# Attention and feed-forward on one core: the last visit four steps sooner, and the rows of the last two chunks spread over nine steps

## The chip, the cores and the metric

One core of a Trainium2 chip runs the whole program. The metric is the device time in microseconds (us) of one execution. Engines are named as in the profile: PE is TensorE, DVE is VectorE, ACT is ScalarE, POOL is GpSimd, and SP is the engine whose queue issues most of the DMAs.

## The reference

```
scores = (q @ k.T) / sqrt(64)                 # q, k, v: 8 batches, 8 heads, 576 tokens, 64 wide, fp32
mask   = local (last 32 tokens) for heads 0-3; strided (same position mod 32) for heads 4-7
attn   = softmax(where(mask, scores, -1e9)) @ v
x      = attn.transpose(0, 2, 1, 3).reshape(8, 576, 512)
xn     = (x - mean(x)) / sqrt(var(x) + 1e-6) * g_ln
out    = x + relu(xn @ w_ch1) @ w_ch2         # w_ch1 512x2048, w_ch2 2048x512
```

## The kernel before

The 4608 tokens are cut into nine chunks of 512: chunk b (0 to 7) is the first 512 tokens of batch b, chunk 8 is the 64 left over from each batch. Every matmul of the feed-forward part is done as three fp32r products of a high and a low part (`xh`, `xl`; `hh`, `hl`).

A chunk goes through 16 **steps** f = 0 to 15, one for each 128 of the 2048 hidden columns. In step f, PE does `ffn1` (12 products of 128x512 into the one PSUM bank `ph`), and then the two halves of `ffn2` of step f-1 (12 products into the four sums `po`). ACT makes `hh` from `ph` and DVE makes `hl` from `ph` and `hh`. As there is one `ph` bank, `ffn1` of step f+1 can start once `hl` of step f is made. Each engine executes in the order in which the program was written: the last lines of the kernel chain every instruction to the one before it on its engine.

Attention runs beside this, in **visits** that a generator hands out between `ffn1` and `ffn2`. A pair of heads takes three visits: scores and values (`sv` on PE; mask, maximum and the values' scaling `xo` on DVE; the store of `xo` to the DRAM rows `xdl` and `xds`; a round trip through DRAM in blocks, `sp` and `sx`), then the load of a later `v`, then the turn of the blocks (`pt<-sp` on DVE and others). `slots` says which steps hand out a visit: three of four, all but f % 4 = 1, and one more at f = 9 of the last run. Pair 31, the last, has its one visit in step 11 of the last run (chunk 6), and its store is the last attention result.

Chunks 7 and 8 are then done together in eight **double steps** (`two_steps`) by a scheme of seven products over sums and differences of the two chunks (`t1` to `t4`, `b22`) and of weight blocks (`s` forms, made on POOL by `s_raws`). What it needs is prepared by `coming` within the last steps of chunk 6: load the rows of the two chunks (`x_load`), normalise them (`x_normed`: per tile of 128 rows `bn_stats` and `bn_aggr` on DVE; one power on POOL for all; then one scaling per tile on ACT), turn them on PE into a PSUM bank of a ring of three (`x_turn`, tile `px`), and form the high and low parts (`turn_seventh` for chunk 7, `turn_last` for chunk 8, `more_forms`).

```
at = 2 * f + end - 2 * LAST          # LAST = 11; end is 0 ahead of ffn2, 1 at the step's end
1: free_attention()   2: all 24 loads   3: x_normed(chunk 7)
5: turn_seventh(0, 1), x_normed(chunk 8)      6: turn_seventh(2, 3), s_forms(0)
7: turn_last(0, 1)    8: turn_last(2, 3)      9: more_forms()
```

Of the kernel before, what the change touches and what calls it, by code (L numbers as in the profile page):

```python
# [8 lines left out]
F32 = mybir.dt.float32  # L9
# [3 lines left out]
AF = mybir.ActivationFunctionType  # L13
# [33 lines left out]
def kernel(  # L47
# [10 lines left out]
    nc = tc.nc  # L58
# [46 lines left out]
            tc.tile_pool(name="ps_o", bufs=2, space=bass.MemoryType.PSUM, side="right")))  # L105


    KEPT = 44
    LATE = 120

    ident = keep.tile([P, P], F32, name="ident")
# [634 lines left out]
    def x_t(c):  # L746
        if c not in xt:
            n = c % 2 if c < 2 else (c + 1) % 2
            xt[c] = tuple(xtp.tile([P, NCC, CH], F32R, tag=f"{t}{n}", name=f"{t}{c}")
                          for t in ("xh", "xl"))  # L750
        return xt[c]
# [7 lines left out]
    def x_load(c, i, t=None, halves=(0, 1)):  # L759

        if t is None:
            t = tkp.tile([P, DM], F32, tag="tk", name=f"x{c}_{i}")
        if c < B:
            parts = [(0, P, c, P * i)]
        else:
            parts = [(REST * j, REST, 2 * i + j, CH) for j in range(2)]
        for p0, n, b, r in parts:
            if 0 in halves:
                nc.sync.dma_start(t[p0:p0 + n, 0:DM // 2], xd_l[b][r:r + n, :])
            if 1 in halves:  # L770
                xs = xd_s[b][0:S].rearrange("(r t) d -> t r d", t=NB)
                nc.sync.dma_start(t[p0:p0 + n, DM // 2:DM], xs[r // STR:(r + n) // STR])
        return t
# [8 lines left out]
        nc.gpsimd.tensor_tensor(out=rs, in0=rs, in1=mhalf, op=ALU.pow)  # L782
        return rs

    def x_normed(c, xs):

        mv = stp.tile([P, NT, 2], F32, tag="mv4", name=f"mv{c}", bufs=1)
        rs = stp.tile([P, NT], F32, tag="rs4", name=f"rs{c}", bufs=2)
        for i, x in enumerate(xs):
            st = stp.tile([P, 6], F32, tag="st", name=f"st{c}_{i}")  # L790
            nc.vector.bn_stats(st, x)
            nc.vector.bn_aggr(mv[:, i], st)
        nc.vector.tensor_scalar(rs, mv[:, :, 1], 1e-6, None, op0=ALU.add)
        nc.gpsimd.tensor_tensor(
            out=rs, in0=rs, in1=mhalf.broadcast_to([P, NT]), op=ALU.pow)
        for i, x in enumerate(xs):
            nc.scalar.activation(out=x, in_=x, func=AF.Copy, scale=rs[:, i:i + 1])

    def x_turn(x, name):
        ps = fresh_bank(f"px{name}").rearrange("p (c x) -> p c x", c=NCC)  # L800
        for cc in range(NCC):
            nc.tensor.transpose(ps[:, cc, :], x[:, cc * P:(cc + 1) * P], ident)
        return ps
# [41 lines left out]
    class Run:  # L845
# [11 lines left out]
        def residual(self, f):  # L857

            if not self.last:
                return  # L860
            if self.c < 2:
                i = f - (NFC - NT - 3)
                loads, scales = [i] * (0 <= i < NT), [i - 2] * (1 < i <= NT + 1)
            elif self.c < PLAIN - 1:
                loads = {1: [0], 5: [1], 9: [2], 10: [3]}.get(f, [])
                scales = {5: [0], 9: [1], 13: [2, 3]}.get(f, [])
            else:
                loads = {9: [0], 10: [1], 11: [2], 12: [3]}.get(f, [])
                scales = {11: [0, 1], 13: [2, 3]}.get(f, [])
            for i in loads:  # L870
                x = x_load(self.c, i)
                if self.first:
                    t = None
                else:
                    t = tkp.tile([P, DM], F32, tag="tk", name=f"t{self.c}_{i}")
                    nc.sync.dma_start(t, part[P * i:P * (i + 1), :])
                self.xres.append([x, t])
            for i in scales:
                r = self.xres[i]
                x, t = r  # L880
# [203 lines left out]
    def free_attention():  # L1084
        attn_ctx.close()
        bank_ctx.close()
        pool = late["pool"] = ctx.enter_context(tc.tile_pool(name="late", bufs=1))
        pool.tile([P, LATE], F32, name="late_pad")
        ps_c = ctx.enter_context(tc.tile_pool(name="ps_c", bufs=1, space=bass.MemoryType.PSUM))
        fresh[:] = [(ps_c, f"c{i}") for i in range(3)]  # L1090
        for n in ("t1h", "t1l", "t2h", "t2l"):
            late_tile(n, n)
        late["x"] = []
        for n in ("b22h", "b22l"):
            x = late_tile(n, "x" + n, F32)
            late["x"] += [x[:, 0], x[:, 1]]

    def late_tile(tag, name, dtype=F32R, shape=(P, 2, CH)):
        t = late[name] = late["pool"].tile(list(shape), dtype, tag=tag, name=name)
        return t  # L1100
# [3 lines left out]
    def row_tile(name):  # L1104
        n_rows[0] += 1
        return late_tile(f"r{n_rows[0] % NT}", name, F32, (P, DM))
# [6 lines left out]
    def sub(engine, out, a, b, op=ALU.subtract):  # L1113
        engine.tensor_tensor(out=out, in0=a, in1=b, op=op)  # L1114

    def raw(t):
        return t.bitcast(F32)

    def high_low(hi, lo, src, engine=nc.vector):
        nc.scalar.activation(out=hi, in_=src, func=AF.Copy)  # L1120
        sub(engine, lo, src, raw(hi))

    def turn_seventh(i):
        xh, xl = x_t(B - 1)
        cs = quarter[i]
        high_low(xh[:, :, cs], xl[:, :, cs], x_turn(late["x"][i], f"{B - 1}_{i}"))

    def turn_last(i):
        xh, xl = (raw(t)[:, 0:2, quarter[i]] for t in x_t(B - 1))
        px = x_turn(late["xr"][i], f"{B}_{i}")  # L1130
        t = late["xr"][i].rearrange("p (n c x) -> p n c x", n=2, c=2)
        late["ts"] += [[t[:, 0], t[:, 1]]]
        t1, t2 = late["ts"][i]
        h = [late[n + "h"][:, :, quarter[i]] for n in ("t1", "t2", "b22")]
        l = [late[n + "l"][:, :, quarter[i]] for n in ("t1", "t2", "b22")]
        nc.scalar.activation(out=h[2], in_=px[:, 2:4], func=AF.Copy)
        sub(nc.vector, t1, px[:, 0:2], xh)
        sub(nc.vector, t1, t1, xl)
        sub(nc.vector, t2, px[:, 2:4], t1)
        nc.scalar.activation(out=h[0], in_=t1, func=AF.Copy)  # L1140
        nc.scalar.activation(out=h[1], in_=t2, func=AF.Copy)
        for k, src in ((2, px[:, 2:4]), (0, t1), (1, t2)):
            sub(nc.vector, l[k], src, raw(h[k]))

    def more_forms():

        xh, xl = x_t(B - 1)
        late["t3"], late["t4"] = x_t(B)
        for i in range(NT):
            t1, t2 = late["ts"][i]  # L1150
            cs = quarter[i]
            h, l = (raw(x)[:, :, cs] for x in (xh, xl))
            sub(nc.vector, t1, t2, h[:, 0:2])
            sub(nc.vector, t1, t1, l[:, 0:2])
            sub(nc.gpsimd, t2, h[:, 2:4], t2)
            sub(nc.gpsimd, t2, t2, l[:, 2:4], ALU.add)
        for n, k, engine in (("t3", 0, nc.vector), ("t4", 1, nc.gpsimd)):
            for i in range(NT):
                cs = quarter[i]
                high_low(late[n][:, 0:2, cs], late[n][:, 2:4, cs], late["ts"][i][k], engine)  # L1160

    def coming(f, end):

        at = 2 * f + end - 2 * LAST
        if at == 1:
            free_attention()
        elif at == 2:
            for i, x in enumerate(late["x"]):
                x_load(B - 1, i, x)
            late["xr"] = [x_load(B, i, row_tile(f"xr{i}")) for i in range(NT)]  # L1170
            late["ts"] = []
        elif at == 3:
            x_normed(B - 1, late["x"])
        elif at == 5:
            turn_seventh(0)
            turn_seventh(1)
            x_normed(B, late["xr"])
        elif at == 6:
            turn_seventh(2)
            turn_seventh(3)  # L1180
            late["s"] = s_forms(0)
        elif at == 7:
            for n in ("b22h", "b22l"):
                late_tile(n, n)
            turn_last(0)
            turn_last(1)
        elif at == 8:
            turn_last(2)
            turn_last(3)
        elif at == 9:  # L1190
            more_forms()

    def weight_parts(p):
# [128 lines left out]
        run = two[0].run  # L1322
        return coming_s, [((run, f0, h0), range(NT)), ((run, f1, (hh, hl)), range(NT))]

    LAST = 11
    bank_ctx = ExitStack()
    gen = visits()
    steps = [(r, f) for r in runs for f in range(r.f0, r.f1)]
# [1 line left out]
    slots = {}  # L1330
    for n, (r, f) in enumerate(steps):
        slots[n] = (r is runs[1] and f in (11, 13) or r is runs[2]
                    or r is not runs[1] and (f % 4 != 1 or r is runs[-1] and f == LAST - 2))

    x = hidden[SPLIT - 1]
    prev = runs[0], SPLIT - 1, (x["h"], x["l"])
# [130 lines left out]
```

## Time and profile before

| what | value |
|---|---|
| time, median of 3 runs | 928.41 us (926.06 to 929.92) |
| profiled execution | 929.05 us, its span 927.3 us |
| PE busy | 888.4 us, 96% of the span |
| DVE, ACT, POOL busy | 461.6, 240.3 and 245.0 us |
| granted PE clock, mean of the span | 0.983 |
| chain that ended last | PE 84%, DMA 7%, DVE 2% |

The busy shares are means over the span. In slices of 23 us PE is at 90% or more from the fifth slice to the thirtieth, then at 70, 60, 70 and 60 to 90% in four slices, and again at 90% to near the end. Those four slices are the stage that the change touches.

### The profile page before, as it was taken

The page shows a single profiled execution, that of the slowest core. Times are in us where ns is not written, and L with a number is a line of the kernel's source. Part 1 is how long each engine was busy: PE and PEld are TensorE (multiplying, and loading weights), DVE is VectorE, ACT ScalarE, POOL GpSimd, SP SyncE. Part 2 cuts the span into 40 slices and gives each one's busy share as a digit, 9 for nine tenths or more (in the row PEclk, how much of TensorE's full clock was granted, in tenths as well). Part 3 has the DMA queues.
Part 4 walks back from the last instruction along what each step waited for, and adds up shares of the span by engine and source line. Part 5 has one row for each costly group of instructions (what it writes and reads, how often), then busy time and mean ns, then how long its engine had stood idle before and what let it go on. Part 6 is the DMA issues. An engine that isn't in the chain of part 4 may idle for free.

```text
span 927.3 us, 18356 instructions
## 1 busy us (share of the span) xinstructions
PE 888.4 (96%) x7431; PEld 726.4 (78%) x7431; DVE 461.6 (50%) x859; ACT 240.3 (26%) x429; POOL 245.0 (26%) x301
## 2 busy tenths in 40 slices
PE   6799999999999999999999999999997679999998
PEld 4677888888888888888888888888886458888886
DVE  5886573447744455445554554455434493333300
ACT  4765563112211111111111111111111234333200
POOL 6676385101100000001000100010001458676100
PEclk9999999999999999999999999999998789999999
DMA  9988971247685757575857585756423000000211
GB/s 206 213 184 238 249 204 35 38 102 156 118 160 104 132 92 166 104 132 92 166 104 126 94 157 106 125 97 139 74 70 108 19 26 21 1 0 31 75 49 29
DMA packets 330972, 100.64 MB, mean 109 GB/s; under 512 B 269712, under 2 KB 321800, under 8 KB 330888
## 3 DMA queue, kind: packets, MB, share of 16 engines
q1 hardware_dynamic: 258114, 86.11, 41.7%
q10 hardware_dynamic: 72774, 13.36, 9.5%
q8 instruction: 58, 0.95, 0.4%
q14 instruction: 26, 0.21, 0.1%
HBM read 72.37 MB, written 27.06 MB: 107 GB/s over the span
## 4 chain that ended last, share of the span: by engine, by line
PE 84%; DMA 7%; DVE 2%; SPq 2%; ACT 1%; POOL 1%; issue 1%; POOLq 0%; DVEq 0%; ACTq 0%
PE po L836 39%; PE ph L811 30%; PE u L1234 5%; PE sv L659 4%; PE v L1234 2%; DMA s<-in_moe_w_ch_dram 2%; DMA rows<-in_k_dram 2%; DMA xr<-xds 1%; DVE xr L1114 1%; PE c L1234 1%; DMA v_l<-in_v_dram 1%; POOL sr L1114 1%; DMA x<-xds 1%; PE px L690 1%; DMA v_s<-in_v_dram 0%
## 5 line engine op out<-in xcount | busy, mean ns | idle before, releaser
L836 PE MATMUL po<-w,hh 128*128 128x512 f32 x1024 | 321.2, 395 | 0.7 <-DVE hl L822 0.7
L811 PE MATMUL ph<-xh,w 128*128 128x512 f32 x880 | 292.9, 394 | 1.1 <-DVE hl L822 1.1
L836 PEld LDWEIGHTS po<-w,hh 128*128 128x128 f32 x1024 | 189.9, 188 | 40.5 <-ACT pt L503 0.8
L822 DVE SCALAR_TENSOR_TENSOR hl<-ph,hh 128x512 fp32r<-128x512 f32 x112 | 77.5, 692 | 280.4 <-ACT hh L817 280.4
L836 PE MATMUL po<-w,hl 128*128 128x512 f32 x512 | 200.0, 391 | 0.0
L811 PEld LDWEIGHTS ph<-xh,w 128*128 128x128 f32 x880 | 166.9, 190 | 36.4 <-DVE hl L822 1.5
L811 PE MATMUL ph<-xl,w 128*128 128x512 f32 x440 | 172.4, 392 | 0.0
L817 ACT ACTIVATE hh<-ph 128x512 fp32r<-128x512 f32 x112 | 66.8, 596 | 336.9 <-PE ph L811 265.1
L488 POOL TENSOR_TENSOR sm<-sm,mx 128x640 f32<-128x640 f32 (+1 forms) x32 | 40.7, 1270 | 372.0 <-issue 211.8
L836 PEld LDWEIGHTS po<-w,hl 128*128 128x128 f32 x512 | 96.5, 189 | 20.5
L811 PEld LDWEIGHTS ph<-xl,w 128*128 128x128 f32 x440 | 83.5, 190 | 17.0
L782 POOL TENSOR_TENSOR rs<-rs,mhalf 128x1 f32<-128x1 f32 x28 | 15.4, 551 | 144.6 <-DVE rs L781 117.3
L493 ACT ACTIVATE sm<-sm 128x640 f32<-128x640 f32 (+1 forms) x32 | 23.8, 742 | 105.7 <-POOL sm L488 105.7
L836 PE MATMUL po<-w,h 128*128 128x512 f32 x186 | 42.3, 389 | 0.0
L1114 POOL TENSOR_TENSOR sr<-sr,w 128x256 f32<-128x256 f32 x48 | 40.0, 833 | 3.8
L836 PEld LDWEIGHTS po<-w,h 128*128 128x128 f32 x186 | 34.9, 188 | 7.2
L1114 POOL TENSOR_TENSOR s<-sr,s 128x256 fp32r<-128x256 f32 x32 | 24.4, 794 | 23.3 <-ACT s L1220 23.3
L239 DVE SCALAR_TENSOR_TENSOR p<-s,p 128x512 uint32<-128x512 uint32 x32 | 22.0, 689 | 11.7 <-ACT p L235 11.6
L484 DVE TENSOR_REDUCE mx<-sm 128x10 f32<-128x640 f32 (+1 forms) x32 | 26.3, 822 | 1.9
L1114 DVE TENSOR_TENSOR x<-po,x 128x512 f32<-128x512 f32 x8 | 5.3, 689 | 39.6 <-PE po L836 29.9
L671 DVE TENSOR_TENSOR xo<-sv,den 128x256 f32<-128x256 f32 (+1 forms) x72 | 24.0, 389 | 0.0
L229 ACT ACTIVATE s<-s 128x512 f32<-128x512 f32 x32 | 21.4, 671 | 6.2 <-DMA s<-in_moe_w_ch_dram 6.2
(194 smaller groups left out, 996.4 us busy)
## 6 DMA issues: line engine op xcount, KB each, us to landing
s<-in_moe_w_ch_dram SPq DMA_DIRECT2D x32, 512.0 KB
out_dram<-x SPq DMA_DIRECT2D x32, 256.0 KB
raw<-in_q_dram SPq DMA_DIRECT2D x104, 72.0 KB
raw<-in_k_dram ACTq DMA_DIRECT2D x68, 72.0 KB
xdl<-xo SPq DMA_DIRECT2D x16, 256.0 KB
x<-xdl SPq DMA_DIRECT2D x32, 128.0 KB
x<-xds SPq DMA_DIRECT2D x32, 128.0 KB
wd<-sm SPq DMA_DIRECT2D x10, 384.0 KB
```

Source lines behind the costliest of these rows:

```text
L239: nc.vector.scalar_tensor_tensor(out=self.p[i], in0=self.bits(i), scalar=3, in1=self.p[i], op0=ALU.logical_shift_left, op1=ALU.bitwise_or)
L484: engine(self.mx[:, :, 0:nt], self.smv, axis=AX.X)
L488: nc.gpsimd.tensor_tensor(out=sm, in0=sm, in1=mx[:, :, 0:nt].unsqueeze(3).broadcast_to([P, 2, nt, w]), op=ALU.subtract)
L493: nc.scalar.activation(out=self.smv, in_=self.smv, func=AF.Exp, scale=SCALE)
L659: nc.tensor.matmul(dst, at, by, start=True, stop=True, tile_position=pos)
L671: nc.vector.tensor_tensor(out=xot[0:n, :, t0:t1], in0=src, in1=pv.den[0:n, :, t0:t1].unsqueeze(3).broadcast_to([n, 2, t1 - t0, D]), op=ALU ...
L811: nc.tensor.matmul(ph, w[:, cc], x[:, cc, :], start=(n + k == 0), stop=(n == NCC - 1 and k == 2))
L817: nc.scalar.activation(out=hh, in_=ph, func=AF.Relu)
L822: nc.vector.scalar_tensor_tensor(out=hl, in0=ph, scalar=0.0, in1=hh.bitcast(F32), op0=ALU.max, op1=ALU.subtract)
L836: nc.tensor.matmul(po, hx[:, cs], w, start=(start and n == 0), stop=(stop and n == 2))
L1114: engine.tensor_tensor(out=out, in0=a, in1=b, op=op)
L1234: nc.tensor.matmul(po, a[:, c], b[:, c, :], start=(start and c + k == 0), stop=(stop and c == 1 and k == 2), skip_group_check=True)
```

## The change

`LAST` becomes 7, and the visits that `slots` left out are handed out in the steps behind step 7 of chunk 5 and in all of chunk 6, so pair 31 is visited in step 7. `coming` is spread over steps 3 to 15. Three tiles of chunk 8 (batches 0 to 5) are loaded in steps 3 to 5 and normalised at the end of step 6; the local halves of three more tiles are loaded in step 6; what needs the last store is loaded at the end of step 7; the fourth tile of chunk 8 and the four of chunk 7 are normalised together at the end of step 10. Chunk 8 is turned first and copied by ACT to the row tiles `ts`; `turn_seventh` then forms its sums and differences with chunk 7's `px` in PSUM as one operand.

```diff
-    KEPT = 44
+    KEPT = 36
...
             else:
-                loads = {9: [0], 10: [1], 11: [2], 12: [3]}.get(f, [])
-                scales = {11: [0, 1], 13: [2, 3]}.get(f, [])
+                loads = {7: [0], 9: [1], 14: [2, 3]}.get(f, [])
+                scales = {13: [0, 1], 15: [2, 3]}.get(f, [])
...
+    def turn_last(i):
+        px = x_turn(late["x8"][i], f"{B}_{i}")
+        h, l = (late["b22" + k][:, :, quarter[i]] for k in "hl")
+        nc.scalar.activation(out=h, in_=px[:, 2:4], func=AF.Copy)
+        nc.scalar.copy(out=late["ts"][i], in_=px.rearrange("p (n c) x -> p n c x", n=2))
+        sub(nc.vector, l, px[:, 2:4], raw(h))
...
-        xh, xl = x_t(B - 1)
         cs = quarter[i]
-        high_low(xh[:, :, cs], xl[:, :, cs], x_turn(late["x"][i], f"{B - 1}_{i}"))
...
+        px = x_turn(late["x"][i], f"{B - 1}_{i}")
+        xh, xl = (t[:, :, cs] for t in x_t(B - 1))
+        t1, t2 = (late["ts"][i][:, n] for n in range(2))
+        h, l = ([late[n + k][:, :, cs] for n in ("t1", "t2")] for k in "hl")
+        nc.scalar.activation(out=xh, in_=px, func=AF.Copy)
+        sub(nc.vector, t1, t1, px[:, 0:2])
+        sub(nc.vector, t2, t2, t1)
         nc.scalar.activation(out=h[0], in_=t1, func=AF.Copy)
         nc.scalar.activation(out=h[1], in_=t2, func=AF.Copy)
-        for k, src in ((2, px[:, 2:4]), (0, t1), (1, t2)):
-            sub(nc.vector, l[k], src, raw(h[k]))
+        sub(nc.vector, xl, px, raw(xh))
+        sub(nc.vector, l[0], t1, raw(h[0]))
+        sub(nc.vector, l[1], t2, raw(h[1]))
+        sub(nc.vector, t1, t2, px[:, 0:2])
+        sub(nc.vector, t2, px[:, 2:4], t2)
...
     def more_forms():
-            sub(nc.vector, t1, t2, h[:, 0:2])
-            sub(nc.vector, t1, t1, l[:, 0:2])
-            sub(nc.gpsimd, t2, h[:, 2:4], t2)
-            sub(nc.gpsimd, t2, t2, l[:, 2:4], ALU.add)
...
-        at = 2 * f + end - 2 * LAST
...
+        at = f + 0.5 * end - LAST
...
+        if at == -4:
+            late["x8"] = tiles(NT, f"x{B}")
+            late["x"] = tiles(2, f"x{B - 1}")
+        elif at in (-3.5, -2.5, -1.5):
+            i = int(at + 3.5)
+            x_load(B, i, late["x8"][i])
+        elif at == -1:
+            for i, x in enumerate(late["x"]):
+                x_load(B - 1, i + 2, x, (0,))
+            x_load(B, NT - 1, late["x8"][NT - 1], (0,))
+        elif at == -0.5:
+            x_normed("a", late["x8"][0:3])
+        elif at == 0.5:
             free_attention()
+            x_load(B, NT - 1, late["x8"][NT - 1], (1,))
+            for i, x in enumerate(late["x"]):
+                x_load(B - 1, i, x, (0, 1) if i < 2 else (1,))
...
+        elif at == 3.5:
+            x_normed("b", late["x8"][3:] + late["x"])
...
-    LAST = 11
+    LAST = 7
...
-                    or r is not runs[1] and (f % 4 != 1 or r is runs[-1] and f == LAST - 2))
+                    or r is not runs[1] and (
+                        f % 4 != 1 or r is runs[-1] or r is runs[-2] and f > LAST))
```

The turns: `turn_last(0)` and `(1)` at the start of step 9, `(2)` in 10, `(3)` with `turn_seventh(0)` in 12, `turn_seventh(1)` at the end of 12, `(2)` with `s_forms(0)` in 13, `(3)` in 14, `more_forms` in 15. The raw forms `sr` of `s_forms` share their SBUF space with the first two tiles of chunk 7 (`xs`).

On ACT, before, steps 12 to 14 of chunk 6 (`hh_12` to `hh_14`; `xb22h` and `xb22l` hold the four tiles of chunk 7, `xr` those of chunk 8):

```order
L817 ACTIVATE hh_12_7714<-ph_12_7701 128x512
L797 ACTIVATE xb22h<-xb22h,rs_7762 128x512 x2
L797 ACTIVATE xb22l<-xb22l,rs_7762 128x512 x2
L817 ACTIVATE hh_13_7794<-ph_13_7781 128x512
L1120 ACTIVATE xh_7824<-px_0_7826 128x4x128
L1120 ACTIVATE xh_7824<-px_1_7833 128x4x128
L797 ACTIVATE xr_7726<-xr_7726,rs_7841 128x512
```

On ACT, now, steps 10 to 12 (`x_3_7308` is the fourth tile of chunk 8; `xs` and the two behind it are chunk 7):

```order
L818 ACTIVATE hh_10_7707<-ph_10_7694 128x512
L1127 ACTIVATE b22h<-px_2_7711 128x2x128
L1128 COPY xr_7599<-px_2_7711 128x512
L798 ACTIVATE x_3_7308<-x_3_7308,rsb 128x512
L798 ACTIVATE xs_7607<-xs_7607,rsb 128x512
L798 ACTIVATE xs_7608<-xs_7608,rsb 128x512
L798 ACTIVATE x_0_7309<-x_0_7309,rsb 128x512
L798 ACTIVATE x_1_7310<-x_1_7310,rsb 128x512
L818 ACTIVATE hh_11_7768<-ph_11_7755 128x512
L818 ACTIVATE hh_12_7797<-ph_12_7784 128x512
```

The scalings stood in two groups of four ahead of `hh_13` and `hh_14`; the second group now is five long and stands ahead of `hh_11`.

On DVE, before, from the turn of pair 31's blocks (`pt`) in step 10 to the last visit's scaling (`xo`) in step 11:

```order
L573 RECIPROCAL den_3_7588<-den_3_7588 128x12
L737 STREAM_TRANSPOSE pt_3_7592<-sp_3_7522 128x768
L822 SCALAR_TENSOR_TENSOR hl_11_7624<-ph_11_7609,hh_11_7622 128x512
L671 TENSOR_TENSOR xo_3_7649<-sv_3_7626,den_3_7588 128x2x3x64
L671 TENSOR_TENSOR xo_3_7649<-sv_3_7626,den_3_7588 128x2x2x64
```

On DVE, now, the same place in steps 6 and 7 (`sta` and `mva` are the statistics of three tiles of chunk 8):

```order
L573 RECIPROCAL den_3_7487<-den_3_7487 128x12
L737 STREAM_TRANSPOSE pt_3_7491<-sp_3_7416 128x768
L792 BN_STATS sta_7511<-x_0_7305 128x6
L793 BN_AGGR mva<-sta_7511 128x2
L792 BN_STATS sta_7514<-x_1_7306 128x6
L793 BN_AGGR mva<-sta_7514 128x2
L792 BN_STATS sta_7517<-x_2_7307 128x6
L793 BN_AGGR mva<-sta_7517 128x2
L794 TENSOR_SCALAR rsa<-mva 128x3
L823 SCALAR_TENSOR_TENSOR hl_7_7540<-ph_7_7525,hh_7_7538 128x512
L671 TENSOR_TENSOR xo_3_7565<-sv_3_7542,den_3_7487 128x2x3x64
```

The statistics of three tiles now stand between the turn and `hl` of the next step, ahead of the last visit's `xo`.

On SP's queue, now, from the last store `xds_218<-xo` in step 7 (`x_0_7583` is a residual row tile of chunk 6):

```order
L554 DMA xds_218<-xo_3_7565 54x5x128
L769 DMA x_0_7583<-xdl_209 128x256
L772 DMA x_0_7583<-xds_217 128x1x256
L772 DMA x_3_7308<-xds_217 64x1x256
L772 DMA x_3_7308<-xds_218 64x1x256
L769 DMA xs_7607<-xdl_210 128x256
L772 DMA xs_7607<-xds_218 128x1x256
L769 DMA xs_7608<-xdl_210 128x256
L772 DMA xs_7608<-xds_218 128x1x256
L772 DMA x_0_7309<-xds_218 128x1x256
L772 DMA x_1_7310<-xds_218 128x1x256
```

Before, the same store was followed by one residual tile, 8 loads of chunk 7 and 16 of chunk 8; now 8 loads of the two chunks stand behind it.

## Rows read from the trace of the kernel before

**Rows 1.** Busy time by stretch: steps 13 to 15 with the first double step; the second.
```profile
core 0: us, PE busy (x) PEld busy (x) DVE busy (x) ACT busy (x) POOL busy (x), PEclk, DMA share, GB/s
703.87:769.38 65.51, 44.32 (x159) 33.80 (x158) 38.17 (x75) 21.56 (x48) 30.65 (x40) 0.79 0.14 48
769.38:784.37 14.99, 14.99 (x68) 12.39 (x66) 5.00 (x7) 5.49 (x11) 11.24 (x15) 1.00 0.01 2
```

**Rows 2.** Timeline of PE: start, us, instruction, count, [idle before and its releaser].
```profile
694.73 0.92 PE L659 MATMUL sv<-v_s,pt 54*64 54x64 f32 x44
...
714.17 1.97 PE L802 MATMUL px<-ident,xb22h 128*128 128x128 f32 x8 [4.70 <-ACT xb22h L797]
...
726.58 0.66 PE L802 MATMUL px<-ident,xb22l 128*128 128x128 f32 x4 [4.45 <-DVE xl L1114]
727.00 1.03 PE L836 MATMUL po<-w,hh 128*128 128x512 f32 x2
...
730.72 0.63 PE L836 MATMUL po<-w,hh 128*128 128x512 f32 x2
...
741.66 1.03 PE L802 MATMUL px<-ident,xr 128*128 128x128 f32 x8
742.45 0.71 PE L836 MATMUL po<-w,hh 128*128 128x512 f32 x2
...
747.09 0.47 PE L1234 MATMUL c<-xh,w 128*128 128x512 f32 x1 [1.66 <-ACT t2h L1141]
...
758.91 0.80 PE L1234 MATMUL u<-t2h,s 128*128 128x512 f32 x1 [3.84 <-ACT p L1239]
...
762.57 2.93 PE L1234 MATMUL u<-xh,s 128*128 128x512 f32 x6 [0.73 <-ACT u L1239]
```

**Rows 3.** The chain that ended last, around the last visit: start, us, what.
```profile
692.08 2.73 PE ph L811 x12
694.83 0.61 ACT hh L817
...
696.07 1.08 DVE xo L671 x3
...
697.51 3.40 DMA xds<-xo
...
705.95 6.35 DMA xr<-xds
```

**Rows 4.** Timeline of DVE, steps 10 to 15 and the first double step.
```profile
690.09 0.69 DVE L822 SCALAR_TENSOR_TENSOR hl<-ph,hh 128x512 fp32r<-128x512 f32 x1 [4.75 <-ACT hh L817]
...
691.93 0.98 DVE L737 STREAM_TRANSPOSE pt<-sp 128x768 f32<-128x768 f32 x1
...
727.04 0.68 DVE L791 BATCH_NORM_STATS2 st<-xr 128x6 f32<-128x512 f32 x1
...
730.60 0.17 DVE L793 TENSOR_SCALAR rs<-mv 128x4 f32<-128x4 f32 x1
734.97 0.69 DVE L822 SCALAR_TENSOR_TENSOR hl<-ph,hh 128x512 fp32r<-128x512 f32 x1 [4.20 <-ACT hh L817]
...
740.09 0.45 DVE L1114 TENSOR_TENSOR xr<-xr,xl 128x256 f32<-128x256 f32 x1
...
750.58 0.96 DVE L1114 TENSOR_TENSOR xr<-xr,xh 128x256 f32<-128x256 f32 x1
```

**Rows 5.** Timeline of ACT, the scaling of chunk 8's four tiles.
```profile
731.90 2.56 ACT L797 ACTIVATE xr<-xr,rs 128x512 f32<-128x512 f32 x4 [14.49 <-POOL rs L794]
```

**Rows 6.** Timeline of POOL: powers of one and of four columns, and two subtractions.
```profile
718.31 0.55 POOL L782 TENSOR_TENSOR rs<-rs,mhalf 128x1 f32<-128x1 f32 x1 [4.95 <-DVE rs L781]
...
730.84 1.02 POOL L794 TENSOR_TENSOR rs<-rs,mhalf 128x4 f32<-128x4 f32 x1 [4.22 <-DVE rs L793]
...
738.84 3.00 POOL L1114 TENSOR_TENSOR s<-sr,s 128x256 fp32r<-128x256 f32 x4
750.42 0.84 POOL L1114 TENSOR_TENSOR xr<-xh,xr 128x256 f32<-128x256 f32 x1 [8.58 <-issue]
```

**Rows 7.** Timeline of SP's queue: one load's issue.
```profile
701.38 0.52 SPq L772 DMA_DIRECT2D xb22h<-xds  x1
```

More of the change, by code (lines that the diff above doesn't have):

```diff
@@ L783, in x_scale, with x_normed @@
         return rs
-    def x_normed(c, xs):
-        mv = stp.tile([P, NT, 2], F32, tag="mv4", name=f"mv{c}", bufs=1)
-        rs = stp.tile([P, NT], F32, tag="rs4", name=f"rs{c}", bufs=2)
+    def x_normed(name, xs):
+        n = len(xs)
+        mv = stp.tile([P, NT + 1, 2], F32, tag="mv5", name=f"mv{name}", bufs=1)
+        rs = stp.tile([P, NT + 1], F32, tag="rs5", name=f"rs{name}", bufs=2)
         for i, x in enumerate(xs):
-            st = stp.tile([P, 6], F32, tag="st", name=f"st{c}_{i}")
+            st = stp.tile([P, 6], F32, tag="st", name=f"st{name}_{i}")
             nc.vector.bn_stats(st, x)
             nc.vector.bn_aggr(mv[:, i], st)
-        nc.vector.tensor_scalar(rs, mv[:, :, 1], 1e-6, None, op0=ALU.add)
+        nc.vector.tensor_scalar(rs[:, 0:n], mv[:, 0:n, 1], 1e-6, None, op0=ALU.add)
         nc.gpsimd.tensor_tensor(
-            out=rs, in0=rs, in1=mhalf.broadcast_to([P, NT]), op=ALU.pow)
+            out=rs[:, 0:n], in0=rs[:, 0:n], in1=mhalf.broadcast_to([P, n]), op=ALU.pow)
         for i, x in enumerate(xs):
@@ L1090, in free_attention @@
         fresh[:] = [(ps_c, f"c{i}") for i in range(3)]
-        for n in ("t1h", "t1l", "t2h", "t2l"):
+        late["ts"] = [row_tile(f"xr{i}").rearrange("p (n c x) -> p n c x", n=2, c=2)
+                      for i in range(NT)]
+        for n in ("t1h", "t1l", "t2h", "t2l", "b22h", "b22l"):
             late_tile(n, n)
[L1093 to L1096, printed above, removed]
+        late["x"][0:0] = [late_tile(f"s{i}", f"xs{i}", F32, (P, DM)) for i in range(2)]
     def late_tile(tag, name, dtype=F32R, shape=(P, 2, CH)):
@@ L1128, in turn_last @@
[L1128 to L1139, printed above, removed]
+        px = x_turn(late["x"][i], f"{B - 1}_{i}")
@@ L1145, in more_forms @@
+        sub(nc.vector, l[0], t1, raw(h[0]))
+        sub(nc.vector, l[1], t2, raw(h[1]))
+        sub(nc.vector, t1, t2, px[:, 0:2])
+        sub(nc.vector, t2, px[:, 2:4], t2)
     def more_forms():
-        xh, xl = x_t(B - 1)
         late["t3"], late["t4"] = x_t(B)
[L1149 to L1152, printed above, removed]
-            sub(nc.vector, t1, t2, h[:, 0:2])
-            sub(nc.vector, t1, t1, l[:, 0:2])
-            sub(nc.gpsimd, t2, h[:, 2:4], t2)
-            sub(nc.gpsimd, t2, t2, l[:, 2:4], ALU.add)
@@ L1159, in more_forms, with tiles @@
                 cs = quarter[i]
-                high_low(late[n][:, 0:2, cs], late[n][:, 2:4, cs], late["ts"][i][k], engine)
+                high_low(late[n][:, 0:2, cs], late[n][:, 2:4, cs], late["ts"][i][:, k], engine)
     def coming(f, end):
-        at = 2 * f + end - 2 * LAST
-        if at == 1:
+        at = f + 0.5 * end - LAST
+        def tiles(n, name):
+            return [tkp.tile([P, DM], F32, tag="tk", name=f"{name}_{i}") for i in range(n)]
+        if at == -4:
[11 more added lines that the diff above has]
+        elif at == 0.5:
             free_attention()
+            x_load(B, NT - 1, late["x8"][NT - 1], (1,))
+            for i, x in enumerate(late["x"]):
+                x_load(B - 1, i, x, (0, 1) if i < 2 else (1,))
         elif at == 2:
[L1168 to L1171, printed above, removed]
+            turn_last(0)
+            turn_last(1)
         elif at == 3:
-            x_normed(B - 1, late["x"])
+            turn_last(2)
+        elif at == 3.5:
+            x_normed("b", late["x8"][3:] + late["x"])
         elif at == 5:
+            turn_last(3)
             turn_seventh(0)
+        elif at == 5.5:
             turn_seventh(1)
-            x_normed(B, late["xr"])
         elif at == 6:
             turn_seventh(2)
-            turn_seventh(3)
             late["s"] = s_forms(0)
         elif at == 7:
[L1183 to L1186, printed above, removed]
+            turn_seventh(3)
         elif at == 8:
-            turn_last(2)
-            turn_last(3)
-        elif at == 9:
             more_forms()
```

## The prediction

> **What bounds the kernel now.** I first read the busy shares: PE works for 96% of the span, so time can only be won where PE waits or runs slowly. The slices of the span put that in one place, the last steps of chunk 6 and the first double step. There I took the busy time by stretch, from the first product of step 13 to the first of the second double step, and then PE's timeline for the waits in it. The reader is to see two things. The stretch takes 65.51 us, at a mean granted clock of 0.79; the double step behind it takes 14.99 us, PE is busy for all of it and the clock is 1.00 [rows 1]. And the long waits of PE end on work of `coming`: 4.70 us for chunk 7's scaled tiles, 4.45 us for a PSUM bank that DVE had not read out, 3.84 us for an ACT copy queued behind the high parts of `more_forms` [rows 2].
>
> How much is there to win? Twelve products take 2.73 us [rows 3]. Three steps are six such groups, 16.4 us. Eight turned tiles take 0.40 us each: two of them start at 741.66 and the next product at 742.45 [rows 2]. The first double step has 12 products fewer than the second, 14.99 - 2.73 = 12.3 us [rows 1]. Together 31.9 us at full clock, so the stretch loses 65.5 - 31.9 = **33.6 us**, in waits and in clock.
>
> What starts it all is the last store: `xds<-xo` follows its `xo` at once and takes 3.40 us, and a load of rows issued at 705.95 takes 6.35 us more [rows 3]. Statistics, power, scaling, turning and forming then follow one another while PE has nothing else.
>
> **The change part by part.** The visits keep their number and their work on PE, and the last one comes four steps, some 22 us, sooner. The loads, the turns and the formings keep their sizes; DVE loses eight 256-wide subtractions and gains four, POOL loses eight, ACT gains four copies of 512. These lie beside 5.5 us of products a step and cost nothing as long as `hl` of each step is made in time, for that is what the next `ffn1` waits for. So I look at each step for what now stands ahead of `hh` on ACT and of `hl` on DVE. Let E be the end of a step's `ffn1`. Undisturbed, `hh` (0.61) and `hl` (0.69) are done at E + 1.34, counting the small gaps [rows 3, 4].
>
> *The normalising as a chain.* For four tiles it is to be read whole: statistics from 727.04 to 730.77, power 1.02, scaling 2.56, then `hh` and `hl`, which ends at 735.66 [rows 4 to 6]: 8.6 us. Per tile that is 0.89 on DVE and 0.64 on ACT, plus 0.16 on POOL for each column (0.55 for one, 1.02 for four). Three tiles make 2.84 + 0.87 + 1.92 + 1.30 = 6.9 us, five make 4.62 + 1.18 + 3.20 + 1.30 = 10.3 us, from the first statistic to the end of the next step's `hl`.
>
> *Three tiles, end of step 6.* They begin when the turn of pair 31's blocks is over. That turn ends at 692.91, 2.13 us after its step's `hl` (690.78) [rows 4]. So `hl` of step 7 is done at E + 1.34 + 2.13 + 6.9 = E + 10.4. PE needs it at E + 3 x 2.73 + 0.92 (the last `sv` [rows 2]) = E + 9.1. **New wait at step 8: 1.3 us.** The last `xo` stands behind this `hl` and is late by nearly as much.
>
> *Five tiles, end of step 10.* They begin behind one low part of 0.45 [rows 4], so `hl` of step 11 is done at E + 1.8 + 10.3 = E + 12.1. PE needs it at E + 3 x 2.73 + 0.4 = E + 8.6. **New wait at step 12: 3.5 us.** It is the wait of before in a smaller form: the five scalings stand ahead of `hh` of step 11 in ACT's order.
>
> *The clock behind it.* After the wait of 4.45 us PE's rows stay long until 730.72, and the granted clock of the stretch says why: the lower of its two levels, 1.2 GHz for 2.4. 4.1 us at half speed lose **2.1 us**. After 1.66 us the row is not long (0.47 against 0.80 behind 3.84 us) [rows 2]. So I charge it behind the 3.5 us and not behind the 1.3 us. Bounds: 0, and twice that, for behind 758.91 the rows are long still past the next wait (2.93 for six at 762.57).
>
> *Forming, steps 12 and 13.* Let T be the end of `ffn1` of step 12. DVE owes `hl` (T + 1.34), a low part and two `turn_seventh` of one 512-wide (0.69) and six 256-wide (0.45) subtractions each, 3.4 us a tile, before `hl` of step 13, which so ends at T + 9.3. PE needs it at T + 3 x 2.73 + 4 x 0.4 = T + 9.8. There is no wait if nothing is slower. But POOL makes the raw forms at that very time, because their space is freed when chunk 7's first tiles are turned. With POOL busy, one subtraction of two SBUF operands took 0.96 (beside POOL's row at 750.42), another 0.45 (within POOL's row at 738.84) [rows 4, 6]. Six of the fourteen have two SBUF operands. At +0.5 each that is 3.0 - 0.5 = 2.5 us of wait; at none, 0. I take the middle, **1.2 us**, as the rows show both.
>
> The Trainium skill (SBUF — State Buffer, section "SBUF: two separate sides") says that DVE with two SBUF inputs and POOL share a port pair as an exclusive lock, held for a whole instruction. The row of 0.96 agrees with it; by that rule the 0.45 should not stand where it does. By the rule alone the term would be 2.5 or more in place of 1.2; its worst case is a rival below.
>
> *The first double step.* Its 3.84 us go: the copy `p` stood behind POOL's and DVE's extra forms, which are now done at `turn_seventh`. The 0.73 us for the copy of `u` stay, since nothing is put between them [rows 2]: **0.7 us**.
>
> *Late rows.* From E of step 6: `xo` and the store's issue at E + 11.8, landed at + 3.4, eight loads of 0.54 each behind it, the last landed 6.35 later [rows 3, 7]: E + 26.0. The five statistics run from E + 26.7 to E + 31, the last tile's from E + 30. They are covered, with some 4 us to spare.
>
> **The sum.** 1.3 + 3.5 + 2.1 + 1.2 + 0.7 = 8.8 us stay of 33.6, so 24.8 us go. The profiled execution took 929.05 us, 0.6 us above the median of the runs shown: 929.05 - 24.8 = 904.2, by the median 903.6. I say **904 us**; with the bounds of the clock and of the forming, 900 to 908.
>
> **The rivals.** (A) is that forecast.
>
> (B) The normalising is hidden: no wait at steps 8 and 12. 904.2 - 1.3 - 3.5 - 2.1 = 897. For it speaks that DVE and ACT are half idle; against it, that ACT's order holds `hh` behind the scalings and that in the kernel before just this chain is seen in full.
>
> (C) By the rule on the port pair each of the six subtractions waits for a whole instruction of POOL, 0.84: 5.0 - 0.5 = 4.5 us at step 14 and 2.1 for the clock, in place of 1.2: 910. Against it is the row of 0.45.
>
> (D) The rows come late: from 4 us of delay on, each us is one of wait at step 12. Loads that need twice 6.35 us give 2 to 6 us: 906 to 910. Against it, 10 loads now stand behind the store instead of 26.
>
> (E) The other side: visits three steps apart. From pair 26 to 31 five intervals lose a step. The block round trip (`sp`, for pairs 26 and 27 `sx` as well) and the q and k loads must land in that much less; if not, DVE waits in front of `pt` and `hl` is behind it. From 5 us a pair, about 3 of wait and 2.1 of clock, the 24.8 us are gone: 929 or more. Against it: pair 31 already follows pair 30 after three steps, and its `pt` starts without a wait at 691.93 [rows 4]; that interval has no `sx` and no loads, though. In part, 1 to 2 us a pair, it gives 909 to 914.
>
> That the last visit does not come sooner is excluded by the order of the instructions.
>
> **How the numbers follow.** Chances: A 0.60, B 0.12, C 0.07, D 0.07, E in part 0.09, E in full 0.05. The range 896 to 911 takes in A, B, C, D and a little of E. About 0.5%, 4.6 us, is what a measurement of this kernel can tell from no change (its three runs lie 3.9 us apart). All but E in full are faster by more: faster 0.95; of the rest, same 0.02, slower 0.03.
>
> **What would show it.** Right: in the profile after, PE has a wait of about 1.3 us for `hl` at step 8 and one of 3 to 4 us at step 12, rows of half speed behind the second only, no wait on `px` for PSUM or for scaled tiles, and 0.7 us at `u` in the first double step. Step by step: ACT scales five tiles directly ahead of `hh` of step 11. Wrong: statistics that wait for a DMA at the end of step 10 (D), subtractions of 1 us or more beside POOL and a wait at step 14 over 2.5 us (C), PE waiting at `sv` or for `hl` in chunk 5 (E), or no wait at step 12 at all (B). If the double steps behind the first grow longer than 14.99 us, the change has cost where I saw none.

## The result and the profile after

The changed kernel took 914.0 us (median of 4 runs, 912.42 to 916.03) against 928.61 (926.06 to 929.92): ratio 0.985, 95% interval 0.9815 to 0.9879. It is faster by 14.6 us, not by the 24.8 us forecast, and lies outside the range. The profiled execution is the slowest of the four (916.03, span 914.2).

First the stretches: three behind the waits outside the tail, then step 13 to the end of the first double step, then the second. They are the busy times by stretch (columns as in [rows 1]).

```profile
621.93:626.00 4.07, 4.07 (x11) 3.26 (x12) 3.97 (x10) 0.63 (x1) 0.00 (x0) 0.59 0.81 127
689.03:693.50 4.47, 4.47 (x13) 3.52 (x14) 0.93 (x3) 0.00 (x0) 0.00 (x0) 0.62 0.37 100
717.23:721.30 4.07, 4.07 (x11) 3.21 (x12) 0.00 (x0) 0.00 (x0) 0.00 (x0) 0.58 0.00 0
725.65:756.38 30.73, 30.00 (x137) 24.42 (x136) 23.85 (x52) 13.70 (x33) 20.56 (x28) 1.00 0.15 52
756.38:771.37 14.99, 14.99 (x68) 12.41 (x67) 5.16 (x7) 5.60 (x12) 11.24 (x16) 1.00 0.01 2
```

The stretch that took 65.51 us [rows 1] now takes 30.73, at full clock: of PE's waits nothing is left in it but 0.73 us. (2.4 us of the difference are six turned tiles that now stand ahead of it, at the 0.40 us each of the prediction.) The second double step is unchanged at 14.99. So the gain was had, and part of it given back earlier. PE's waits after the first 100 us (us in total, times, longest) say where:

```profile
PE ph L812 <- DVE hl L823: 9.2, 3, 3.8
PE u L1242 <- ACT u L1247: 0.7, 1, 0.7
```

And PE's timeline gives the places (columns as in [rows 2]): in front of step 14 of chunk 5 and of steps 8 and 12 of chunk 6, with the first product of step 14 behind them.

```profile
621.93 0.79 PE L812 MATMUL ph<-xh,w 128*128 128x512 f32 x1 [2.25 <-DVE hl L823]
...
689.03 0.50 PE L812 MATMUL ph<-xh,w 128*128 128x512 f32 x1 [3.81 <-DVE hl L823]
...
717.23 0.65 PE L812 MATMUL ph<-xh,w 128*128 128x512 f32 x1 [3.14 <-DVE hl L823]
...
731.71 0.40 PE L812 MATMUL ph<-xh,w 128*128 128x512 f32 x1
```

All three long waits are for `hl`, and behind each some 4 us run at a granted clock of about 0.6, part of the time at the lower of the two levels (1.2 GHz for 2.4). Duration times one minus the clock prices that: 4.07 x 0.41, 4.47 x 0.38 and 4.07 x 0.42, 1.7 us each. So 9.2 + 5.1 = 14.3 us stand outside the stretch.

What held `hl` is read one engine back, on ACT, which makes `hh` ahead of it:

```profile
611.62 0.60 ACT L818 ACTIVATE hh<-ph 128x512 fp32r<-128x512 f32 x1 [1.53 <-PE ph L812]
614.91 5.54 ACTq L419 DMA_DIRECT2D v_s<-in_v_dram  x6
620.56 0.60 ACT L818 ACTIVATE hh<-ph 128x512 fp32r<-128x512 f32 x1 [8.34 <-DMA sp<-wd]
...
685.83 1.95 ACT L798 ACTIVATE x<-x,rsa 128x512 f32<-128x512 f32 x3 [9.14 <-POOL rsa L795]
687.68 0.57 ACT L818 ACTIVATE hh<-ph 128x512 fp32r<-128x512 f32 x1
...
712.80 0.72 ACT L798 ACTIVATE x<-x,rsb 128x512 f32<-128x512 f32 x1 [5.97 <-POOL rsb L795]
713.43 1.32 ACT L798 ACTIVATE xs<-xs,rsb 128x512 f32<-128x512 f32 x2
714.66 1.32 ACT L798 ACTIVATE x<-x,rsb 128x512 f32<-128x512 f32 x2
715.88 0.57 ACT L818 ACTIVATE hh<-ph 128x512 fp32r<-128x512 f32 x1
```

At steps 8 and 12 it is the scalings, directly ahead of `hh`, as foreseen. In chunk 5 it is something else: six v loads that ACT itself issues ahead of `hh` of step 13. The first goes out at 614.91, 2.7 us after the `hh` of 611.62 is done, and the six take 5.54 us. The issues themselves are short, as the trace's account of line 419 there shows (in ns, least, median and most; then the first and last start, in us):

```profile
L419 ACTq DMA_DIRECT2D v_s<-in_v_dram x6: 279/280/337, 614.9 to 620.2; - x6
```

That is some 1.7 us of the 5.54. The rest is waiting: by the semaphore events of the trace each issue was released by the landing of a load of the same visit's blocks, an `sx` load for the first four and an `sp` load for the last two. In ACT's order `hh` stands behind the last of them.

Such a group isn't new, nor is its length. ACT before, in chunk 4:

```profile
475.95 0.60 ACT L817 ACTIVATE hh<-ph 128x512 fp32r<-128x512 f32 x1 [4.84 <-PE ph L811]
476.22 5.16 ACTq L419 DMA_DIRECT2D v_s<-in_v_dram  x6
481.48 0.60 ACT L817 ACTIVATE hh<-ph 128x512 fp32r<-128x512 f32 x1 [4.94 <-PE ph L811]
```

There the six took 5.16 us, but they began while the `hh` ahead of them was still at work, and the next `hh` was 0.1 us late. In chunk 5 `hh` is 3.5 us late (idle 8.34 us for 4.84), and 2.7 of these are the late start.

Why step 8 waits 3.81 us and not 1.3 is seen on DVE and on SP's queue. DVE first:

```profile
680.59 0.70 DVE L792 BATCH_NORM_STATS2 sta<-x 128x6 f32<-128x512 f32 x1 [0.26 <-DMA x<-xdl]
...
683.74 0.69 DVE L792 BATCH_NORM_STATS2 sta<-x 128x6 f32<-128x512 f32 x1 [2.24 <-DMA x<-xds]
...
688.28 0.69 DVE L823 SCALAR_TENSOR_TENSOR hl<-ph,hh 128x512 fp32r<-128x512 f32 x1 [3.42 <-ACT hh L818]
```

The statistics of the second and third x8 tile waited 0.26 and 2.24 us for their rows. SP's queue shows where the loads had stood:

```profile
671.77 2.03 SPq L722 DMA_DIRECT2D sp<-wd  x4
673.85 0.54 SPq L769 DMA_DIRECT2D x<-xdl  x1
...
677.67 0.53 SPq L772 DMA_DIRECT2D x<-xds  x1
```

SP issues in the order of the program. The eight loads of those two tiles, from 673.85 to 678.2, stand behind the `sp` loads of pair 30's visit in step 4, which read pair 31's blocks and had to wait for them to be stored. Nothing in those rows depends on it. The last of the eight goes out at 677.67, and its statistic starts at 683.74.

### The profile page after: what moved, and what is told of

Read it like the earlier page. It is cut to its first block, busy times and chain, and to the rows that moved or that the text cites. A ratio compares the mean times of both kernels' runs of the same rounds, so it can differ in the third digit from the quotient of the medians.

```text
span 914.2 us, 18339 instructions
## 1 busy us (share of the span) xinstructions
PE 885.7 (97%) x7431; PEld 725.0 (79%) x7431; DVE 455.6 (50%) x855; ACT 241.8 (26%) x433; POOL 238.6 (26%) x293
## 4 chain that ended last, share of the span: by engine, by line
PE 87%; issue 5%; DMA 3%; SPq 2%; ACT 2%; DVE 1%; POOL 0%; ACTq 0%; DVEq 0%; POOLq 0%
PE po L837 40%; PE ph L812 30%; PE u L1242 5%; PE sv L659 4%; PE v L1242 2%; PE c L1242 1%; SPq L722 1%; DMA x<-xds 1%; PE px L690 1%; DMA rows<-in_k_dram 1%; PE av L514 1%; PE pp L498 1%; PE av L523 0%; DMA sp<-wd 0%; PE t L377 0%
## 5 line engine op out<-in xcount | busy, mean ns | idle before, releaser
L292 POOL TENSOR_TENSOR w<-r,w 128x512 fp32r<-128x512 f32 x16 | 20.6, 1294 | 8.4 <-ACT w L288 8.3
```

## The experiments

The first four kernels below stand beside 7 runs of the kernel before (928.61 us, 927.69 to 932.95), the last three beside 11 more (928.56 us, 925.70 to 931.29). A ratio is to that kernel before.

**e1_again.** The changed kernel once more, not a character altered.

> The changed kernel itself, a second time, for a second profile. In the first one TensorE stood idle in the first 35 us for 2.57 and 4.17 us in the middle of a run of equal matmuls, with no releaser, and the steps of chunk 1 came about 4 us later than in the kernel before, though nothing was changed there. Theory 1 (this differs from execution to execution): here the steps of chunk 1 come at another time, by 2 us or more, and the time lies near 912 to 916. Theory 2 (it belongs to the changed program): the same two idle times, the steps again 4 us late.

912.22 us (909.07 to 913.59, 4 runs), ratio 0.9808 (0.9777 to 0.9839). The profiled execution took 909.07, 7 us less than the first one. It has the same three waits, of 2.54, 3.28 and 3.15 us; but the busy times by stretch behind them (columns as above) show the slow clock behind the third alone:

```profile
617.29:621.40 4.11, 3.97 (x88) 3.03 (x88) 4.01 (x10) 1.23 (x2) 0.00 (x0) 1.00 0.79 126
682.47:687.00 4.53, 4.53 (x20) 3.74 (x21) 1.63 (x4) 0.60 (x1) 0.00 (x0) 1.00 0.38 101
709.08:713.20 4.12, 4.12 (x10) 3.29 (x11) 0.00 (x0) 0.00 (x0) 0.00 (x0) 0.50 0.00 0
```

That is some 3 us of the 7: 5.1 against 4.12 x 0.50 = 2.1. Most of the rest lies in the first 35 us, where the first trace has PE idle in the middle of equal matmuls with no releaser:

```profile
19.02 0.31 PE L445 MATMUL sp<-kt_l,qt_l 64*32 64x64 f32 x1 [2.57 <-issue]
...
31.38 0.65 PE L514 MATMUL av<-v_l,pt 64*32 64x65 f32 x21 [4.17 <-issue]
```

The second execution of the same program has 0.30 us at the first place and nothing at the second:

```profile
17.68 0.24 PE L445 MATMUL sp<-kt_l,qt_l 64*32 64x64 f32 x1 [0.30 <-issue]
```

So this idle, and the clock behind the first two waits, belong to an execution, not to the change. The other kernels below have 0.55 to 2.59 us at the first place. The variants are compared with 912.2.

**e2_rows_early.** The twelve loads of the first three x8 tiles are asked for at the end of step 3, ahead of pair 30's loads in SP's queue.

```
-        elif at in (-3.5, -2.5, -1.5):
-            i = int(at + 3.5)
-            x_load(B, i, late["x8"][i])
+        elif at == -3.5:
+            for i in range(3):
+                x_load(B, i, late["x8"][i])
```

> The 12 loads of the first three tiles of chunk 8 are all issued at the end of step 3, ahead of the visit of step 4 on SP's queue, in place of one tile each at the ends of steps 3, 4 and 5. Theory (the second and third tile stood behind that visit's block loads on SP and landed after their statistics were due): no statistic waits for a DMA at the end of step 6, the wait at step 8 falls from 3.8 to 1.3 to 1.5 us and no slow rows follow it: 3.5 to 4 us faster than the changed kernel. Rival (the loads land late whatever stands ahead of them, or the wait at step 8 is the scaling's alone): the wait stays above 3 us, no gain.

907.54 us (905.70 to 907.59, 4 runs), ratio 0.9758 (0.9731 to 0.9784). DVE's second and third statistic follow the first without a wait, and PE's wait at step 8 falls from 3.28 to 1.13 us; first DVE, then PE:

```profile
674.21 0.70 DVE L792 BATCH_NORM_STATS2 sta<-x 128x6 f32<-128x512 f32 x1
...
675.04 0.66 DVE L792 BATCH_NORM_STATS2 sta<-x 128x6 f32<-128x512 f32 x1
```

```profile
680.30 0.50 PE L812 MATMUL ph<-xh,w 128*128 128x512 f32 x1 [1.13 <-DVE hl L823]
```

With the rows in time, the wait is the prediction's own: 1.3 us forecast, 1.13 measured, at full clock. The edit moves the time by 4.7 us; 2.15 of that is the wait, and the rest may be the clock behind it, slow in some executions of the changed kernel and not in others.

**e3_v_on_sp.** All v loads that ACT issued go out on SP's queue. The edit takes in more than the stall: 18 groups, the first at 262 us in the trace before, and not the last visits alone. PE waited at none of the other 17.

```
-                pairs[i + 2].load_v(queue=nc.scalar if by_blocks else nc.sync)
+                pairs[i + 2].load_v(queue=nc.sync)
```

> The loads of v in the last visits are issued from SP's queue and not from ScalarE's. Theory (in chunk 5 hh of step 13 stood behind six DMA issues of ScalarE that took 5.5 us, as they now come one step behind the block loads and wait for them): the wait of 2.25 us in chunk 5 and the slow rows behind it go, 4 us faster than the changed kernel. Rival (the visits are too close for their block loads or their q and k loads, so VectorE is late in front of pt or of the transposes): the wait stays or comes elsewhere in chunk 5.

908.19 us (907.74 to 908.99, 4 runs), ratio 0.977 (0.9745 to 0.9795): 4.0 us less than e1_again. PE does not wait in chunk 5, and ACT's `hh` there is released by PE, 4.84 us after ACT fell idle, as it is where nothing disturbs it:

```profile
612.97 0.60 ACT L818 ACTIVATE hh<-ph 128x512 fp32r<-128x512 f32 x1 [4.84 <-PE ph L812]
```

The six issues of that visit take 2.43 us on SP, and no wait of PE follows them. The waits at steps 8 and 12 stay (3.42 and 3.15 us).

**e4_scale_later.** The scalings are called behind the `hh` of steps 7 and 11.

```
     def x_normed(name, xs):
...
+        def scale():
+            for i, x in enumerate(xs):
+                nc.scalar.activation(out=x, in_=x, func=AF.Copy, scale=rs[:, i:i + 1])
+        return scale
...
-            x_normed("a", late["x8"][0:3])
+            late["scale"] = x_normed("a", late["x8"][0:3])
+        elif at in (0, 4):
+            late["scale"]()
...
-            x_normed("b", late["x8"][3:] + late["x"])
+            late["scale"] = x_normed("b", late["x8"][3:] + late["x"])
```

> Only the place of the scalings on ScalarE changes: both groups stand behind hh of the next step (steps 7 and 11) and not ahead of it; statistics and power stay. Theory (hh of the next step is held by the scalings behind it in ScalarE's order): the wait at step 12, 3.1 us, and its slow rows go; of the wait at step 8, 3.8 us, at most 0.5 stays, that of hl behind the late statistics on VectorE. About 9 to 10 us faster than the changed kernel, 904 to 906. Rival (the wait is set by the statistics on VectorE): each of the two waits loses less than half.

902.71 us (900.80 to 903.07, 4 runs), ratio 0.9704 (0.9673 to 0.9735): 9.5 us less than e1_again, as much as expected, and below 904 to 906, which was counted from the slower first runs. Both waits of chunk 6 are gone, though the rows of the third x8 tile are still late: with `hh` ahead of the scalings, nothing that PE needs soon stands behind them. PE's wait in chunk 5 stays:

```profile
620.85 0.50 PE L814 MATMUL ph<-xh,w 128*128 128x512 f32 x1 [2.11 <-DVE hl L825]
```

**e7_five_scalings_later.** Of e4, only the second half: the five scalings move, the three stay.

```
-            x_normed("a", late["x8"][0:3])
+            x_normed("a", late["x8"][0:3])()
...
-            x_normed("b", late["x8"][3:] + late["x"])
+            late["scale"] = x_normed("b", late["x8"][3:] + late["x"])
+        elif at == 4:
+            late["scale"]()
```

> The changed kernel with only the five scalings of the second normalising moved, from ahead of the hh of step 11 to behind it; the three of the first stay. If the wait at step 12 is made by the five scalings, as the prediction had it, PE's 3.15 us there and the 1.7 us of slow rows behind them go, and the wait at step 8 stays at 3 to 4 us: 912.2 - 4.8 = 907.4 (906 to 909). If it is the five statistics ahead of hl that hold it, 2 us or more of the wait stay and the time is 910 or above.

906.56 us (905.21 to 908.29, 5 runs), ratio 0.9767 (0.9745 to 0.9788): 5.7 us less than e1_again. The wait at step 12 is gone, those in chunk 5 and at step 8 stay:

```profile
616.76 0.50 PE L814 MATMUL ph<-xh,w 128*128 128x512 f32 x1 [2.30 <-DVE hl L825]
...
683.42 0.80 PE L814 MATMUL ph<-xh,w 128*128 128x512 f32 x1 [3.55 <-DVE hl L825]
```

The five statistics still stand ahead of `hl` on DVE and cost PE nothing. The scalings ahead of `hh` were the cause. The three at step 8 are the rest of e4: 9.5 - 5.7 = 3.8 us.

**e6_visits_alone.** The other way round: the kernel before, with the visits four steps sooner and nothing else.

```
-                    or r is not runs[1] and (f % 4 != 1 or r is runs[-1] and f == LAST - 2))
+                    or r is not runs[1] and (
+                        f % 4 != 1 or r is runs[-1] or r is runs[-2] and f > 7))
```

> The kernel before, with the visits of chunks 5 to 7 four steps sooner and nothing else: rows are loaded, scaled, turned and formed as before, from step 12 on. It measures what the earlier visits cost and bring by themselves. By the finding that six v loads ahead of hh on ACT stall chunk 5: a wait of about 2.3 us in front of ffn1 of step 13 there, with 2 us of slow rows, 4.3 us in all. By the prediction's view of the visits, no wait in chunk 5. Both: the 26 loads of rows no longer stand behind the last store, so the wait of 4.70 us for the scaled tiles [rows 2] shrinks or goes, and the order of normalising, turning and forming keeps most of the other 28 us. So with the stall 924 to 930, without it 920 to 926; the wait in chunk 5 tells them apart, the time alone does not.

920.15 us (917.02 to 922.17, 6 runs), ratio 0.9909 (0.9887 to 0.9931), below the 924 to 930 that went with a stall; the stall is there all the same. PE's timeline:

```profile
617.41 0.64 PE L811 MATMUL ph<-xh,w 128*128 128x512 f32 x1 [2.52 <-DVE hl L822]
...
723.59 0.66 PE L802 MATMUL px<-ident,xr 128*128 128x128 f32 x4 [2.05 <-ACT xr L797]
727.23 1.11 PE L802 MATMUL px<-ident,xr 128*128 128x128 f32 x4 [2.98 <-DVE xl L1114]
...
737.99 0.47 PE L1234 MATMUL c<-xh,w 128*128 128x512 f32 x1 [2.15 <-ACT t2h L1141]
...
749.82 0.50 PE L1234 MATMUL u<-t2h,s 128*128 128x512 f32 x1 [3.86 <-ACT p L1239]
```

The wait of 2.52 us in chunk 5 (for `hl` of step 13, in front of step 14) is made by the earlier visits alone. For the rest, I had undersized what earlier rows are worth: not only the 4.70 us for chunk 7's scaled tiles is gone but the 4.45 us for the bank too. PE still waits for chunk 8's tiles, 2.05 us for the scaling and 2.98 for a bank, and 2.15 and 3.86 us in the double step. So the visits alone bring 8.4 us net of their stall; the spreading takes these waits away and brings the rest.

**e5_all_three.** The edits of e2, e3 and e4 in one kernel; the v loads on SP are all those of e3.

> The three edits together: loads of the first three x8 tiles asked for at the end of step 3, pair 28's and later v loads on SP, scalings behind the hh of steps 7 and 11. If the three waits are separate costs, the time is that of the run with later scalings, 902.7, less the 4.0 us that v on SP gave (912.2 - 908.2): 898.7, 897 to 901, and no wait of PE over 1 us after 100 us. The early rows add nothing, since with the scalings behind hh nothing of PE waits for those rows. The rival: the stall of chunk 5 is only moved, to be given back in the next wait; then 902 to 903.

**896.68 us** (896.32 to 896.95, 5 runs), ratio 0.9659 (0.9638 to 0.968), 32 us below the kernel before and below the forecast. All that is left of PE's waits after the first 100 us:

```profile
PE u L1246 <- ACT u L1251: 0.7, 1, 0.7
```

It is 2 us below the sum of the separate edits, less than the runs of e1_again (4.5 us) and of e4 (2.3 us) lie apart. The three stalls are separate costs, none given back elsewhere.

## Why the prediction was wrong

| term, us | forecast | profile after | change of the median by the run that takes it away |
|---|---|---|---|
| visits in chunk 5 | 0 | 2.25 + 1.7 clock | e3: 4.0 |
| wait at step 8 | 1.3, no clock | 3.81 + 1.7 clock | e2: 4.7, with 1.13 of wait left; e4 less e7: 3.8 |
| wait at step 12 | 3.5 + 2.1 clock | 3.14 + 1.7 clock | e7: 5.7 |
| forming, step 14 | 1.2 | 0 | not tried |
| first `u` | 0.7 | 0.73 | not tried |
| sum | 8.8 | 15.0 | |

904.2 - 8.8 + 15.0 = 910.4. The profiled execution took 916.03; 3.9 us of the 5.6 between are the idle in the front (by 119.26 us it was that much behind the kernel before), and 1.7 us I can't place. The second execution of the same program lost less: 9.0 of long waits, 2.1 of clock and 0.7, which gives 904.2 - 8.8 + 11.8 = 907.2. It took 909.07, so again 1.9 us are not placed.

**The stretch and what goes from it: right.** Nearly all of the 33.6 us went, and the long waits of [rows 2] with them; 0.73 us of wait are left.

**The step that failed: the visits.** "The visits keep their number and their work on PE" is true, and the wrong thing to count: a visit also puts up to six DMA issues into ACT's stream, ahead of `hh`, and the prediction put nothing for them. With a step less between visits these issues come right behind the loads of `sx` and `sp`, on whose landings they wait: they start 2.7 us late and end 5.54 us after that. Had they started at once, `hh` would have been 0.8 us late, and PE bears 1.3 (3.5 - 2.25). This last is an estimate from the rows above; no run moves the start alone. What the runs show is that the earlier visits by themselves make the stall (e6: 2.52 us of wait) and that it goes with the issues (e3).

Rival E, visits three steps apart, had the right part of the change, and its sign, PE waiting for `hl` in chunk 5, is in the profile. But it looked for the cause on DVE, in front of `pt`, which waited 0.4 us in the first trace and at most 1.0 in the others. That its price in part, 909 to 914, takes in the measured 914.0 is luck: E counted 1 to 2 us for every pair, and the profile has one stall, in chunk 5, and a second loss at step 8 that E doesn't have.

The Trainium skill (DMA: Bandwidth & Descriptors, section "Issuing engines are not separate DMA queues") says that issuing from several engines only saves the sequencer's time, which is usually small relative to the DMA itself. The trace agrees: an issue took 0.28 to 0.34 us here. What cost 5.54 us on ACT was the waiting ahead of each, and what mattered was whose instructions stood behind it.

**The step that was mis-sized: three tiles at step 8.** The chain was right, its start wrong: "They begin when the turn of pair 31's blocks is over" took it that the rows had landed. I followed the loads behind the last store on SP's queue with care ("Late rows") and not the eight of the first tiles, which stand behind another visit in the same queue. e2 shows the chain as forecast (1.13 us) once they are in time. That no slow rows follow this wait was forecast for a short one; behind the longer one they came in some executions.

**Step 12: right.** 3.14 us for 3.5 with the five scalings ahead of `hh`, half-speed rows behind, and 5.7 us when undone (in runs that lie 3.1 us apart) for 5.6 forecast. No statistic there waited for a DMA, so rival D is out. ("Late rows" left out the two residual loads ahead of the eight, 1.1 us; its 4 us to spare cover them.)

**Forming: the contention came as forecast, the work beside it was over-sized.** No wait stands at step 14. DVE after, from `hl` of step 12 to behind the third `turn_seventh`, and POOL at work on the raw forms beside it, its last row ending at 730.71:

```profile
723.83 0.42 DVE L1114 TENSOR_TENSOR xr<-xr,px 128x256 f32<-128x256 f32 x1
...
727.75 0.55 DVE L1114 TENSOR_TENSOR xr<-xr 128x256 f32<-128x256 f32 x1
...
728.82 0.41 DVE L1114 TENSOR_TENSOR t1l<-xr,t1h 128x256 fp32r<-128x256 f32 x1
729.16 0.96 DVE L1114 TENSOR_TENSOR t2l<-xr,t2h 128x256 fp32r<-128x256 f32 x1
...
730.82 0.68 DVE L823 SCALAR_TENSOR_TENSOR hl<-ph,hh 128x512 fp32r<-128x512 f32 x1
731.42 0.41 DVE L1114 TENSOR_TENSOR xr<-xr,px 128x256 f32<-128x256 f32 x1
...
734.26 0.68 DVE L777 BATCH_NORM_STATS2 st<-x 128x6 f32<-128x512 f32 x1
```

```profile
727.28 0.74 POOL L1114 TENSOR_TENSOR sr<-w,sr 128x256 f32<-128x256 f32 x1
728.10 0.81 POOL L1114 TENSOR_TENSOR sr<-sr,w 128x256 f32<-128x256 f32 x1
728.87 0.97 POOL L1114 TENSOR_TENSOR sr<-w,sr 128x256 f32<-128x256 f32 x1
729.91 0.80 POOL L1114 TENSOR_TENSOR sr<-sr,w 128x256 f32<-128x256 f32 x1
```

The six subtractions of two SBUF operands took 0.50, 0.41, 0.95 us in the first tile and 0.55, 0.41 and 0.96 in the second, which is shown; those with an operand in PSUM take 0.41 to 0.43. The two tiles beside POOL took DVE 3.5 us each (723.83 to 730.82). The third, of the same seven subtractions, took 2.84 (731.42 to 734.26), and POOL's next row starts only at 733.12. So POOL cost some 1.3 us, close to half of the 3.0 that the forecast had at most. But it had 3.4 us for an undisturbed tile: it added the lengths of the rows, and the rows overlap (728.82 + 0.41 is past 729.16). That is 1.1 us too much for two tiles, so the slack was some 1.6 us in place of 0.5, and covered what POOL cost: `hl` of step 13 ends at 731.50, and PE's next product follows at 731.71 without a wait. Rival C is out.

The Trainium skill (SBUF — State Buffer, section "SBUF: two separate sides") has the two engines lock each other out for whole instructions. All six rows agree. The four longer ones began within a row of POOL and end 0.28 us behind its end (727.75 + 0.55 and 727.28 + 0.74; 729.16 + 0.96 and 728.87 + 0.97); the two of 0.41 began less than 0.1 us ahead of the end of one (728.82 and 728.10 + 0.81). In the third tile one began 0.02 us behind the start of a POOL row and took 0.42; there POOL's row is the long one, 1.03 us. So a subtraction waits for the rest of POOL's instruction, not for a whole one. The prediction's row of 0.45, held there against the rule, agrees too: in the trace before it began at 740.09, the row of POOL around it ended at 740.26, and it ended at 740.54.

**Rival B** came true by an edit: with no wait at steps 8 and 12 it gave 897, and e5_all_three, which takes these and the stall in chunk 5 away, took 896.7. The 1.2 us for forming in B's sum were not there, so part of that match is chance.

## What to carry to other kernels

A DMA that a computing engine issues is an instruction in that engine's order: when work is moved closer to what precedes it, count its issues, the landings they wait for and above all how late the first can start, and put them on a queue behind which nothing urgent stands. For every load that is moved earlier, read what stands ahead of it on its in-order queue, not only what it depends on. And work for later (scalings here) goes behind the instruction that the busiest engine waits for, not ahead of it: those two small reorderings and one change of queue were worth 15.5 us here, about as much as the change itself.

## What was not expected of the hardware

The same program, executed twice, had PE idle with no releaser for 6.7 us at two places in the first 35 us in one execution and for 0.3 us in the other. Nothing in the trace says why, and it stays open.

The slow clock behind a wait depends on more than the wait. In chunk 5, with waits of 2.1 to 2.6 us, the granted clock behind them was 0.58 to 0.68 in three traces (the first of the changed kernel, e6, e7) and 1.00 in three (e1, e2, e4), with the same visits in all six. At step 8 it was 0.50 to 0.65 behind 3.42 to 3.81 us in three traces (the first, e3, e7) and 1.00 behind 3.28 in e1. At step 12, behind 3.14 or 3.15 us, it was slow in all four that have that wait: 0.50 to 0.61. So the clock costs 1.3 to 2.2 us if it falls (duration times one minus the clock, 4.14 x 0.32 in e7 to 4.43 x 0.50 in e3), and the price of a wait here is a range, not a number. What decides it the runs don't show.
